# The branch for experts with more than 256 rows, moved from ahead of the last expert to the beginning of the experts

## The chip, the cores and the metric

One NeuronCore of a Trainium2 chip runs the whole program. The metric is the device time of one execution in microseconds (us). The engines are named as the profile names them: PE is TensorE's matmuls and PEld its weight loads (one sequencer issues both), DVE is VectorE, ACT is ScalarE, POOL is GpSimd, SP is SyncE. A "q" behind a name (PEldq, SPq) marks work of that engine's sequencer, such as a branch or a wait, during which the engine itself may go on with what is queued.

## The reference, cut to what matters

Three stages in a row: a blocked linear attention, a gated product of dense matrices, and a top-1 mixture of eight experts on 1536 rows of 512. Only the last one matters here (capacity is 1536 / 8 * 2 = 384 rows for an expert):

```python
for i in range(N):
    e = expert_idx[i]
    if counts[e] < capacity:
        disp[e, counts[e]] = x[i]
        pos[i] = counts[e]; counts[e] += 1; keep[i] = True
h = np.maximum(np.einsum('ecd,edf->ecf', disp, w1), 0.0)
y = np.einsum('ecf,efd->ecd', h, w2)
for i in range(N):
    if keep[i]:
        out[i] = gate_w[i] * y[expert_idx[i], pos[i]]
```

## The kernel before, in words

**Rows and chunks.** An expert may get up to 384 rows, three chunks of 128 (`nch` = 3). The straight path computes the first two chunks of every expert (`nmain` = 2, 256 rows). A branch holds the third chunk of all eight experts: `overflow()` loads the largest count of rows, `cmax`, into a register of every engine, and its body runs only where that is over 256. In the run that is shown the body is not taken. In the body TensorE has, for each of the eight experts, four transposes (L850), 32 matmuls (L863) and 8 matmuls (L876) in plain float32.

**The order is written by hand.** Each engine runs its instructions in the order of the program's text, and waits on semaphores. Around the change the order is this.

1. The last rows of the dense product: `half_b` and `half_a` for blocks 9 to 11 (L807 to L811), with `advance` and `table` hooked in between their matmuls. `advance` steps the routing of a block: its second step adds the block's one-hot rows to `csum` (L609), the third adds to the table of places. `table` turns that into row indices and starts the gathers of the second halves of the rows of experts 0 and 1 (POOL, L708). A hook is called behind the step `fb` of the same number, and there are steps 0 to 7: the hook at 8 in `half_a(NBLK - 2, {8: advance})` is never called, and stands there so that no `advance` runs behind the half.
2. `x2_half(NBLK - 1, ...)` (L812), the last half block, with `dispatch(0, 1, apart=True)` behind its step 6: four transposes on TensorE (L757), whose results ACT rounds to the high part (`xh`, L769) and DVE turns into the low part (`xl`, L770). Then `rows_a` copies and stores the last rows (L636, L637), and POOL gathers the first halves for experts 0 and 1, which wait for that store.
3. The count: one matmul of `ones` with `csum` (L817) and a DVE maximum to `cmax` (L819).
4. The beginning of the experts (L823 to L830): `mm1(e, pr, (2, 3))` is the second half of the inner sum of the first product, 12 matmuls; it runs for `pr` 0 to 3 of expert 0 and 0 to 1 of expert 1, with `dispatch(1, 1)` and `dispatch(0, 0)` between. The other half, `mm1(0, pr, (0, 1))`, is the first thing in the loop over experts and needs `dispatch(0, 0)`.
5. The loop over experts (L887 on): the rest of `mm1`, the dispatch and gathers for the next experts, then the second product with `e2` (L906) for both chunks and a scatter of the rows by POOL (L718).

**The weights** come in a fixed order through four staging buffers (SP's queue, L82), and ACT (L95) and DVE (L97) split each piece into a high and a low part in `run_bg` steps that stand between the matmuls.

**The branch.** On each engine it is a load of `cmax` by the sequencer (L833, TENSOR_LOAD) and a compare and branch (L834). Where the body is not taken, each engine's other side raises the semaphores by what the body would have added: PE and DVE one instruction each, SP one for each of eight DMA semaphores and POOL one for all of its own (INC_SWDGE_SEM), the last two after a wait for what is still in flight on them. In the kernel before it stands ahead of expert 7 (`OVER`, L888).

Of the kernel before, what the change touches and what calls it, by code (L numbers as in the profile page):

```python
# [12 lines left out]
I32 = mybir.dt.int32  # L13
AF = mybir.ActivationFunctionType
ALU = mybir.AluOpType
AX = mybir.AxisListType
PSUM = bass.MemoryType.PSUM

P = 128
# [4 lines left out]
NE = 8  # L24
NC = 6
NBLK = NT // P
# [5 lines left out]
NST = 4  # L32
NW = (2, 1, 1, 1, 1, 1, 1, 1)
HOOK = 6
OVER = 7
LOADS = (1, 2, 2, 2, 2, 2, 2, 0)
TICKS = ((0, 0, 0, 0), (0, 0, 0, 1)) + ((1, 0, 0, 1),) * 6 + ((0, 0, 1, 0),)
XBW = 265
# [3 lines left out]
def tile_moe_chain(ctx, tc, cap, qk, kv, w12, w3i, woi, wgi, e1i, e2i, c32, c16, zero, out):  # L42
    nc = tc.nc
    nch = min(-(-cap // P), NBLK)
# [6 lines left out]
    def pool(name, bufs=1, **kw):  # L51
        return tc.tile_pool(name=name, bufs=bufs, reuse_waits="tile", **kw)

    const = ctx.enter_context(pool("const"))
# [9 lines left out]
    def bank():  # L64
        return ps.tile([P, 512], F32, tag="b", name="bank")
# [140 lines left out]
    def run_bg(n=1):  # L206
        for _ in range(n):
            feed.tick()
# [70 lines left out]
    csum = const.tile([P, NE], F16, name="csum")  # L279
# [14 lines left out]
    def mm3(acc, wh, wl, rh, rl, first, last):  # L294
        nc.tensor.matmul(acc, wh, rl, start=first, stop=False)  # L295
        nc.tensor.matmul(acc, wh, rh, start=False, stop=False)  # L296
        nc.tensor.matmul(acc, wl, rh, start=False, stop=last)  # L297
# [248 lines left out]
    ones = c16_sb[:, 128:256]  # L546
# [24 lines left out]
    def x2_half(blk, cs, hooks={}):  # L571
        g, tb = divmod(blk, 3)
        ts = slice(tb * P, (tb + 1) * P)
        acc = bank()[:, 0 : cs.stop - cs.start]
        for fb in range(8):
            gh, gl = gts[g, fb]
            mm3(acc, gh[:, ts], gl[:, ts], wxh[:, fb, cs], wxl[:, fb, cs], fb == 0, fb == 7)
            if fb in hooks:
                hooks[fb]()
        return acc  # L580
# [53 lines left out]
    def rows_a(blk, acc):  # L634
        row = p2.tile([P, 256], F32, tag="rowa", name="rowa")
        nc.scalar.copy(row, acc)  # L636
        nc.scalar.dma_start(xa_d[blk * P : (blk + 1) * P, :], row)  # L637
# [5 lines left out]
    def advance():  # L643
        for r in list(routing):
            if next(r, 0) == 0:
                routing.remove(r)

    def half_b(blk, hooks={}):
        acc = x2_half(blk, slice(256, 520), hooks)
        if not hooks:  # L650
            advance()
        routing.append(route(blk, acc))
        next(routing[-1])
        if not hooks:
            run_bg(1)

    def half_a(blk, hooks={}):
        acc = x2_half(blk, slice(0, 256), hooks)
        if not hooks:
            advance()  # L660
        rows_a(blk, acc)
        run_bg(1)
# [64 lines left out]
    def gathers(e, half):  # L727
        for s in range(nmain):
            gather(xg[e % 2][s][half], (xa_d, xb_d)[half], s * NE + e)
# [15 lines left out]
    def dispatch(e, half, apart=False):  # L745
        if e not in xd:
            xd[e] = (
                p3.tile([P, 4, nt], F32R, tag="xdh", name="xdh"),
                p3.tile([P, 4, nt], F32R, tag="xdl", name="xdl"),
                p3.tile([P, nmain], F32, tag="gate", name="gate"),  # L750
            )
        xh, xl, gt = xd[e]
        tp = psi.tile([P, 512], F32, tag="i", name="tp") if half else bank()
        tps = [tp[:, 0:nt], bank()[:, 0:nt] if apart else tp[:, nt : 2 * nt]]
        for kk in range(2):
            for s in range(nmain):
                nc.tensor.transpose(  # L757
                    tps[kk][:, s * P : (s + 1) * P],
                    xg[e % 2][s][half][:, kk * P : (kk + 1) * P],
                    ident,  # L760
                )
        k = 2 * half
        if apart:
            parts = [(xh[:, k + n, :], xl[:, k + n, :], tps[n]) for n in range(2)]
        else:
            tp = tp[:, 0 : 2 * nt].rearrange("p (k t) -> p k t", k=2)
            parts = [(xh[:, k : k + 2, :], xl[:, k : k + 2, :], tp)]
        for h, lo, src in parts:
            nc.scalar.copy(h, src)  # L769
            nc.vector.tensor_tensor(lo, src, h.bitcast(F32), op=ALU.subtract)  # L770
        if half:
            for s in range(nmain):
                nc.vector.tensor_copy(gt[:, s : s + 1], xg[e % 2][s][1][:, 264:265])

    def mm1(e, pr, ks):
        xh, xl, _ = xd[e]
        it = e1_it[2 * e + pr // 2]
        feed.need(it, pieces=2 * (pr % 2) + 2)
        if ks[0] == 2:
            accs[e, pr] = bank()[:, 0 : 2 * nt]  # L780
        acc = accs[e, pr]
        for m in range(2):
            hi, lo = (it.by_fb(part, (2 * pr + m) % 4) for part in (it.hi, it.lo))
            o = acc[:, m * nt : (m + 1) * nt]
            for k in ks:
                for w, x in ((hi, xl), (hi, xh), (lo, xh)):
                    nc.tensor.matmul(  # L787
                        o,
                        w[:, k, :],
                        x[:, k, :],  # L790
                        start=m == 0 and k == 2 and x is xl,
                        stop=m == 1 and k == 1 and w is lo,
                        skip_group_check=True,
                    )
        if ks[-1] == 1:
            hh = p3h.tile([P, 2, nt], F32R, tag="hh", name="hh")
            hl = p3h.tile([P, 2, nt], F32R, tag="hl", name="hl")
            acc = accs.pop((e, pr)).rearrange("p (m t) -> p m t", m=2)
            nc.scalar.activation(hh, acc, AF.Relu)  # L799
            nc.vector.scalar_tensor_tensor(  # L800
                hl, acc, 0.0, hh.bitcast(F32), op0=ALU.max, op1=ALU.subtract
            )
            hts[pr] = (hh, hl)
            it.free = pr % 2 == 1
        run_bg(2 if ks[-1] == 1 else 1)

    half_b(NBLK - 3, {8: advance})  # L807
    half_b(NBLK - 2, {4: advance})
    half_b(NBLK - 1, {4: advance})
    half_a(NBLK - 3, {3: advance, 6: advance, 7: table})  # L810
    half_a(NBLK - 2, {8: advance})  # L811
    acc = x2_half(NBLK - 1, slice(0, 256), {HOOK: lambda: dispatch(0, 1, apart=True)})  # L812
    rows_a(NBLK - 1, acc)
    gathers(0, 0)
    gathers(1, 0)
    cnt = bank()[:, 0:NE]
    nc.tensor.matmul(cnt, ones, csum, start=True, stop=True)  # L817
    cmax = const.tile([P, 1], I32, name="cmax")
    nc.vector.tensor_reduce(cmax, cnt, axis=AX.X, op=ALU.max)  # L819

    late.close()
    p3h = ctx.enter_context(pool("p3h", 6, side="right"))
    hts = {}  # L823
    for pr in range(4):
        mm1(0, pr, (2, 3))
        if pr == 1:
            dispatch(1, 1)
    mm1(1, 0, (2, 3))
    dispatch(0, 0)
    mm1(1, 1, (2, 3))  # L830

    def overflow():
        nmax = nc.values_load(cmax[0:1, 0:1], min_val=0, max_val=NT)  # L833
# [50 lines left out]
                    scatter(y, col)  # L884

    ov = ctx.enter_context(pool("ov", side="right")) if nch > 2 else None
    for e in range(NE):  # L887
        if nch > 2 and e == OVER:  # L888
            overflow()
        for pr in range(4):  # L890
            mm1(e, pr, (0, 1) if (e, pr) in accs else (2, 3, 0, 1))
        gt = xd.pop(e)[2]
        if e + 1 < NE:
            if e:
                dispatch(e + 1, 1)
            dispatch(e + 1, 0)
        if e + 2 < NE:
            gathers(e + 2, 1)
            gathers(e + 2, 0)
        for s in range(nmain):  # L900
            acc = bank()
            ss = slice(s * P, (s + 1) * P)
            for fb in range(8):
                it = e2_it[2 * e + fb // 4]
                feed.need(it)
                mm3(  # L906
                    acc,
                    hts[fb // 2][0][:, fb % 2, ss],
                    hts[fb // 2][1][:, fb % 2, ss],
                    it.view(it.hi)[:, fb % 4, :],  # L910
                    it.view(it.lo)[:, fb % 4, :],
                    fb == 0,
                    fb == 7,
                )
                it.free = s == nmain - 1 and fb % 4 == 3
                if fb % 2:
                    run_bg(1)
            y = p3.tile([P, DM], F32, tag="y", name="y", bufs=3)
            cut = DM if (e, s) != (NE - 1, nmain - 1) else DM // 2
            nc.scalar.activation(y[:, 0:cut], acc[:, 0:cut], AF.Copy, scale=gt[:, s : s + 1])  # L920
            if cut < DM:
                nc.vector.tensor_scalar(
                    y[:, cut:], acc[:, cut:], gt[:, s : s + 1], None, op0=ALU.mult
                )
            scatter(y, s * NE + e)
# [69 lines left out]
```

## Time and profile before

| | us |
|---|---|
| median of three runs (513.02 to 513.99) | 513.52 |
| the profiled execution's own time | 516.84 |
| span of its trace, first to last instruction | 514.8 |

Busy time in that span: PE 498.6 us, PEld 468.7, DVE 264.9, ACT 242.9, POOL 128.7. TensorE's granted clock has a mean of 0.997 of full speed.

All times in the rows below are of the profiled execution, counted from the start of its span. A time of a run without the profiler is some 3.3 us under the profiled execution's own, so differences are worked out inside the trace and then set against the median. Matmuls overlap in the records (each is longer than its distance to the next), so what a matmul costs is the distance from start to start.

### The profile page before, as it was taken

The numbers are of one execution on the slowest core, as the hardware profiler recorded it, in microseconds if no ns is written. First come the engines' busy times: TensorE is split into PE (matmuls) and PEld (weight loads), VectorE is DVE, ScalarE is ACT, GpSimd is POOL, SyncE is SP. The second block draws the span as 40 slices with busy tenths as digits, with TensorE's granted clock in tenths as the row PEclk, the third lists the DMA queues.
The fourth block names the chain that finished last, engine by engine and source line by source line (L and its number), as shares of the span: only waits on it lengthen the run. The fifth ranks groups of instructions, "written<-read, shape, count | busy, mean of one in ns | idle before, by whom it ended". The sixth has DMA issues, their size and how long they took to land. (4 is left out here: it accounts for less than half of the span.)

```text
span 514.8 us, 9557 instructions
## 1 busy us (share of the span) xinstructions
PE 498.6 (97%) x3805; PEld 468.7 (91%) x3805; DVE 264.9 (51%) x576; ACT 242.9 (47%) x485; POOL 128.7 (25%) x124
## 2 busy tenths in 40 slices
PE   8999999999999999999999998899999999999993
PEld 4888999999999999999999998789989898989892
DVE  5998875668332223222332563468383746547420
ACT  2697997789311221122112424457464746546310
POOL 4365664545100000000020005405414040410101
PEclk9999999999999999999999999999999999999998
DMA  8999565557801000100010224486666666574200
GB/s 325 413 410 375 155 227 204 189 187 247 320 26 41 1 0 23 43 1 0 23 43 0 88 69 157 162 299 219 214 213 211 224 224 228 177 250 171 83 2 34
DMA packets 24529, 80.80 MB, mean 157 GB/s; under 512 B 3642, under 2 KB 5692, under 8 KB 24480
## 3 DMA queue, kind: packets, MB, share of 16 engines
q1 hardware_dynamic: 18976, 70.35, 38.4%
q0 software_dynamic: 3344, 7.85, 4.8%
q10 hardware_dynamic: 2160, 1.94, 1.1%
q8 instruction: 32, 0.52, 0.4%
q14 instruction: 17, 0.14, 0.1%
HBM read 74.84 MB, written 10.54 MB: 166 GB/s over the span
## 5 line engine op out<-in xcount | busy, mean ns | idle before, releaser
L97 DVE TENSOR_TENSOR wlo<-st,whi 128x512 fp32r<-128x512 f32 x128 | 82.0, 684 | 16.7 <-ACT whi L95 16.7
L295 PE MATMUL bank<-xtl,whi 128*128 128x384 f32 x256 | 87.1, 340 | 0.0
L297 PE MATMUL bank<-xth,wlo 128*128 128x384 f32 x256 | 86.4, 337 | 0.0
L296 PE MATMUL bank<-xth,whi 128*128 128x384 f32 x256 | 85.8, 335 | 0.0
L95 ACT CAST whi<-st 128x512 fp32r<-128x512 f32 x128 | 73.1, 621 | 16.2 <-PE bank L297 10.7
L787 PE MATMUL bank<-xdl,whi 128*128 128x256 f32 x256 | 72.6, 283 | 4.7 <-issue 2.5
L787 PE MATMUL bank<-xdh,whi 128*128 128x256 f32 x256 | 72.2, 282 | 0.0
L787 PE MATMUL bank<-xdh,wlo 128*128 128x256 f32 x256 | 72.1, 282 | 0.0
L143 POOL TENSOR_TENSOR wlo<-t,whi 128x512 fp32r<-128x512 f32 x40 | 51.9, 1298 | 52.1 <-ACT whi L142 46.5
L295 PE MATMUL bank<-wxl,gh 128*128 128x264 f32 (+1 forms) x192 | 55.9, 291 | 0.0
L296 PE MATMUL bank<-wxh,gh 128*128 128x264 f32 (+1 forms) x192 | 54.1, 282 | 0.0
L297 PE MATMUL bank<-wxh,gl 128*128 128x264 f32 (+1 forms) x192 | 54.1, 282 | 0.0
L787 PEld LDWEIGHTS bank<-xdl,whi 128*128 128x128 f32 x256 | 48.4, 189 | 5.6 <-issue 2.7
L564 DVE TENSOR_TENSOR a_sb<-bank,a_sb 128x384 f32<-128x384 f32 x32 | 17.8, 557 | 66.9 <-PE bank L297 66.3
L295 PE MATMUL bank<-wlo,hh 128*128 128x512 f32 x128 | 51.1, 399 | 0.0
L297 PE MATMUL bank<-whi,hl 128*128 128x512 f32 x128 | 50.4, 394 | 0.0
L718 POOL DMA_INDIRECT out_dram<-y,idx x16 | 16.6, 1038 | 134.2 <-ACT y L920 101.1
L296 PE MATMUL bank<-whi,hh 128*128 128x512 f32 x128 | 50.0, 391 | 0.0
L800 DVE SCALAR_TENSOR_TENSOR hl<-bank,hh 128x512 fp32r<-128x512 f32 x32 | 22.1, 690 | 53.3 <-ACT hh L799 45.5
L787 PEld LDWEIGHTS bank<-xdh,whi 128*128 128x128 f32 x256 | 48.3, 189 | 0.3
L787 PEld LDWEIGHTS bank<-xdh,wlo 128*128 128x128 f32 x256 | 48.4, 189 | 0.0
L295 PEld LDWEIGHTS bank<-xtl,whi 128*128 128x128 f32 x256 | 48.1, 188 | 0.0
(109 smaller groups left out, 1006.1 us busy)
## 6 DMA issues: line engine op xcount, KB each, us to landing
st<-e1i SPq DMA_DIRECT2D x32, 512.0 KB
st<-e2i SPq DMA_DIRECT2D x32, 512.0 KB
st<-w3i SPq DMA_DIRECT2D x16, 512.0 KB
st<-w SPq DMA_DIRECT2D x16, 512.0 KB
tqk<-qk SPq DMA_DIRECT2D x8, 768.0 KB
tkv<-kv SPq DMA_DIRECT2D x8, 768.0 KB
st<-woi SPq DMA_DIRECT2D x8, 512.0 KB
out_dram<-zero SPq DMA_DIRECT2D x1, 3072.0 KB
```

The costliest lines, as they stand in the source:

```text
L95: nc.scalar.copy(h, s)
L97: nc.vector.tensor_tensor(lo, s, h.bitcast(F32), op=ALU.subtract)
L143: nc.gpsimd.tensor_tensor(lo, t, h.bitcast(F32), op=ALU.subtract)
L295: nc.tensor.matmul(acc, wh, rl, start=first, stop=False)
L296: nc.tensor.matmul(acc, wh, rh, start=False, stop=False)
L297: nc.tensor.matmul(acc, wl, rh, start=False, stop=last)
L564: nc.vector.tensor_tensor(a_sb, acc, a_sb, op=ALU.mult)
L718: nc.gpsimd.indirect_dma_start(out=out, out_offset=bass.IndirectOffsetOnAxis(ap=idx[:, col : col + 1], axis=0), in_=src, in_offset=None, b ...
L787: nc.tensor.matmul(o, w[:, k, :], x[:, k, :], start=m == 0 and k == 2 and x is xl, stop=m == 1 and k == 1 and w is lo, skip_group_check=True,)
L800: nc.vector.scalar_tensor_tensor(hl, acc, 0.0, hh.bitcast(F32), op0=ALU.max, op1=ALU.subtract)
```

## The change

The count moves up, behind step 2 of `half_a(NBLK - 2)`; by then `csum` has its last addition, which stands in `half_a(NBLK - 3)`. It replaces the hook that is never called. The branch moves from ahead of expert 7 to right behind `rows_a`, ahead of the gathers of the first halves and of all matmuls of the experts; its body is unchanged. Every engine's stream is touched at both places.

```diff
-OVER = 7
...
+    cmax = const.tile([P, 1], I32, name="cmax")
+
+    def count():
+        cnt = bank()[:, 0:NE]
+        nc.tensor.matmul(cnt, ones, csum, start=True, stop=True)
+        nc.vector.tensor_reduce(cmax, cnt, axis=AX.X, op=ALU.max)
+
...
-    half_a(NBLK - 2, {8: advance})
+    half_a(NBLK - 2, {2: count})
     acc = x2_half(NBLK - 1, slice(0, 256), {HOOK: lambda: dispatch(0, 1, apart=True)})
     rows_a(NBLK - 1, acc)
-    gathers(0, 0)
-    gathers(1, 0)
-    cnt = bank()[:, 0:NE]
-    nc.tensor.matmul(cnt, ones, csum, start=True, stop=True)
-    cmax = const.tile([P, 1], I32, name="cmax")
-    nc.vector.tensor_reduce(cmax, cnt, axis=AX.X, op=ALU.max)
-
     late.close()
     p3h = ctx.enter_context(pool("p3h", 6, side="right"))
-    hts = {}
-    for pr in range(4):
...
-    mm1(1, 1, (2, 3))
...
     ov = ctx.enter_context(pool("ov", side="right")) if nch > 2 else None
+    if nch > 2:
+        overflow()
+    gathers(0, 0)
+    gathers(1, 0)
+    hts = {}
+    for pr in range(4):
+        mm1(0, pr, (2, 3))
+        if pr == 1:
+            dispatch(1, 1)
+    mm1(1, 0, (2, 3))
+    dispatch(0, 0)
+    mm1(1, 1, (2, 3))
     for e in range(NE):
-        if nch > 2 and e == OVER:
-            overflow()
         for pr in range(4):
```

## Rows read from the trace of the kernel before

**Rows 1.** The page: busy time, share of the span, instructions of each engine.
```profile
PE 498.6 (97%) x3805; PEld 468.7 (91%) x3805; DVE 264.9 (51%) x576; ACT 242.9 (47%) x485; POOL 128.7 (25%) x124
```

**Rows 2.** Waits of PE from 315 us to the end: total, times, longest (us).
```profile
PE bank L787 <- issue: 2.5, 1, 2.5
```

**Rows 3.** Timeline ahead of expert 7: start, length (us), instruction, idle before.
```profile
482.82 0.39 PE L297 MATMUL bank<-whi,hl 128*128 128x512 f32 x1
...
483.98 0.19 PEld L787 LDWEIGHTS bank<-xdl,whi 128*128 128x128 f32 x1 [1.19 <-PEq L834]
...
484.20 0.28 PE L787 MATMUL bank<-xdh,whi 128*128 128x256 f32 x1
```

**Rows 4.** Timeline ahead of expert 6, at the same place without a branch.
```profile
459.53 0.40 PE L297 MATMUL bank<-whi,hl 128*128 128x512 f32 x1
...
459.88 0.27 PE L787 MATMUL bank<-xdh,whi 128*128 128x256 f32 x1
```

**Rows 5.** Lines L833, L834: minimum/median/maximum ns, first to last start (us).
```profile
L833 PEldq TENSOR_LOAD <-cmax x1: 492/492/492, 478.9 to 478.9; - x1
L834 PEldq COMPARE_BRANCH  x1: 4148/4148/4148, 479.5 to 479.5; - x1
L834 DVEq COMPARE_BRANCH  x1: 72/72/72, 482.3 to 482.3; - x1
L834 POOLq INC_SWDGE_SEM  x1: 1332/1332/1332, 487.8 to 487.8; - x1
```

**Rows 6.** DMA at 304.18:304.21, 320.25:320.28, 478.60:478.65, 481.28:481.33, 484.40:484.43, 491.20:491.23 (packets, MB, share of 16 engines).
```profile
q8 instruction: 1, 0.02, 275.4%
...
q8 instruction: 1, 0.02, 187.5%
...
q8 instruction: 1, 0.02, 129.8%
...
q8 instruction: 1, 0.02, 109.9%
...
q8 instruction: 1, 0.02, 194.2%
...
q8 instruction: 1, 0.02, 217.1%
```

**Rows 7.** Windows: busy us and instructions (x) of PE, PEld, DVE, ACT, POOL; PEclk.
```profile
304.19:314.55 10.36, 10.36 (x92) 10.00 (x90) 4.05 (x18) 2.57 (x7) 4.15 (x5) 1.00 0.43 134
304.19:320.26 16.07, 14.73 (x129) 14.37 (x128) 6.43 (x26) 5.41 (x14) 6.15 (x7) 1.00 0.44 140
478.62:482.83 4.21, 4.21 (x21) 3.42 (x19) 1.99 (x3) 1.99 (x4) 0.98 (x1) 1.00 0.26 93
484.41:491.21 6.80, 6.80 (x59) 6.80 (x58) 2.47 (x4) 1.71 (x3) 0.78 (x1) 1.00 0.07 28
```

**Rows 8.** Timeline of PEld at the new place of the branch.
```profile
313.52 0.25 PEld L757 LDWEIGHTS tp<-c_sb,xgb 128*128 128x128 f32 x2
...
315.89 0.19 PEld L787 LDWEIGHTS bank<-xdl,whi 128*128 128x128 f32 x1 [1.43 <-DVE xdl L770]
```

**Rows 9.** Timeline around the dispatch of expert 0's first half.
```profile
323.59 0.60 PE L757 MATMUL bank<-c_sb,xga 128*128 128x128 f32 x4
...
327.37 0.69 DVE L770 TENSOR_TENSOR xdl<-bank,xdh 128x512 fp32r<-128x512 f32 x1 [4.64 <-issue]
...
328.12 0.39 PE L787 MATMUL bank<-xdl,whi 128*128 128x256 f32 x1 [2.51 <-issue]
```

**Rows 10.** Timeline of POOL: the first gather behind the new place.
```profile
317.93 1.00 POOL L708 DMA_INDIRECT xga<-xa_d,idx  x1 [3.73 <-DMA xa_d<-rowa]
```

**Rows 11.** Timeline and windows on TensorE's clock: the first matmuls, and the end.
```profile
1.19 5.25 PE L325 MATMUL bank<-warm 128*128 128x512 f16 x12 [1.19 <-DVE warm L319]
...
506.80:511.40 4.60, 0.00 (x0) 0.00 (x0) 0.48 (x1) 0.47 (x1) 0.98 (x1) 1.00 0.10 39
...
511.45:514.80 3.35, 0.00 (x0) 0.00 (x0) 0.00 (x0) 0.00 (x0) 0.00 (x0) 0.50 0.00 0
```

More of the change, by code (lines that the diff above doesn't have):

```diff
@@ L810, in tile_moe_chain @@
     half_a(NBLK - 3, {3: advance, 6: advance, 7: table})
-    half_a(NBLK - 2, {8: advance})
+    half_a(NBLK - 2, {2: count})
     acc = x2_half(NBLK - 1, slice(0, 256), {HOOK: lambda: dispatch(0, 1, apart=True)})
     rows_a(NBLK - 1, acc)
-    gathers(0, 0)
-    gathers(1, 0)
-    cnt = bank()[:, 0:NE]
-    nc.tensor.matmul(cnt, ones, csum, start=True, stop=True)
-    cmax = const.tile([P, 1], I32, name="cmax")
-    nc.vector.tensor_reduce(cmax, cnt, axis=AX.X, op=ALU.max)
     late.close()
     p3h = ctx.enter_context(pool("p3h", 6, side="right"))
-    hts = {}
-    for pr in range(4):
[L825 to L829, printed above, removed]
-    mm1(1, 1, (2, 3))
     def overflow():
```

## The prediction, made before the changed kernel ran

> **What bounds the kernel now.** The page comes first: TensorE is busy for 97% of the span and nothing else is near it [rows 1], so a change is worth what it adds to or takes from TensorE's stream. The view of waits says where that stream stands still among the experts: three places only. One wait of 2.5 us [rows 2] is that of `mm1(0, 0, (0, 1))`, which starts at 328.12 because `dispatch(0, 0)` ended its last subtraction then [rows 9]. One of 1.43 us lies ahead of the first `mm1` at 315.89, for `dispatch(0, 1)` [rows 8]. The third is the branch, ahead of expert 7 [rows 3]. The change touches all three.
>
> **What goes: the branch ahead of expert 7.** With the branch, the second matmul of `mm1` starts 484.20 - 482.82 = 1.38 us behind the last matmul of the expert before [rows 3]; at the same place ahead of expert 6 it is 459.88 - 459.53 = 0.35 us [rows 4]. The branch costs 1.03 us there. It is TensorE alone that holds it up: its compare and branch took 4148 ns, DVE's 72 ns [rows 5]. From here to the last matmul TensorE has no other gap, so 1.03 us comes back whole. The other engines' parts at that place lie beside TensorE's work, and their going brings nothing.
>
> **Why TensorE's branch takes 4.15 us.** The sequencer starts it at 479.55 and is through at 483.70. Queue q8 carries single instruction packets of 0.02 MB. Between 304.2 and 320.25 one comes in the time of 129 + 128 = 257 TensorE instructions [rows 6, 7]: a block of some 256 instructions each. At the branch they come out of turn: one at 478.6 (129.8% of 0.05 us times 16 engines = 1.04 us long), one at 481.3, 1.75 us into the branch (0.88 us long, ended 482.2), one at 484.4 (0.93 us), 0.7 us behind the landing [rows 6]. I read it so: the body that is jumped over is longer than what is held, the landing's block is fetched and can be used 1.5 us behind its packet (482.2 to 483.7), and then the block behind it is asked for. The fetch started only when the one of 478.6 could be used (479.65 + 1.5 = 481.2). Ahead of expert 7 most of the 4.15 us is hidden: the load of `cmax` started at 478.9, while the last matmul queued ahead of it started at 482.82 [rows 3, 5], so 3.9 us of 512-column matmuls were in the queue.
>
> [...]
>
> **What comes: the branch at 314 us.** TensorE's sequencer waits for a gather and lets `dispatch(0, 1)`'s transposes go at 313.52 [rows 8]; ahead of the branch are then four transposes and three matmuls, 14 instructions, at most 0.06 us each. So almost nothing is queued when it gets to the branch. The steps:
> - `cmax` is loaded from about 313.8 (313.6 to 314.3), 0.49 us [rows 5]; the branch starts at 314.4 (314.2 to 314.9).
> - First fetch. No packet is under way (304.2, next 320.25 [rows 6]), so it need not wait for another one: 0.7 + 0.93 + 1.52 = 3.15 us, between 3.05 (with the 0.88 us packet) and the measured 4.15. I take 3.15, the composition of the packet at 484.4. Landing at 317.55; the first weight load 0.28 us later (483.70 to 483.98 [rows 3]).
> - Where it lands. Ahead of expert 7, 40 instructions are counted from the packet at 478.62 to the branch [rows 7], about 37 without those that had started; the sequencer is 33 entries ahead of the engine, and a packet follows its request by some 0.6 us, 5 instructions there. The branch is then some 11 instructions into its block (with the two of the branch itself). At the new place 177 instructions lie between the packet at 304.2 and the last matmul ahead (92 + 90, less three under way and the count's pair [rows 7]); 177 - 33 + 2 + 10 = 156. The body is 8 * (4 + 2 * 40) pairs, 1344 instructions (a plain float32 matmul runs as two pairs), and 1371 with waits and branch in the compiled program: 1372 further is five blocks and 92. So the landing moves from 103 to 248. Counted from behind, by the packets at 484.4 and 491.2 (117 instructions between [rows 7]), the old landing is at 112, which makes the new one 257. The end of the block, 256, lies inside that bound. I take the last few instructions of a block, as the mean, 252, says.
> - Second fetch. The block behind is asked for when the landing is reached, and TensorE has no more than a few instructions until it is there: another 3.15 us (0.7 + 0.93 + 1.52), to 320.7. `mm1` runs from 320.75 instead of 315.89: 4.86 us late, 4.4 at the least and 6.3 at the most with the bounds above.
> - What hides it. Of this, the wait at 328.12 takes 2.51 us [rows 9]: the next 9.7 us of matmuls need nothing new but `dispatch(0, 0)`, whose transposes (323.59) move along to 328.4; with 0.6 us for the transposes, 0.6 for ACT and 0.69 for DVE its parts are there at about 330.4, when `mm1(1, 1)` ends (325.6 + 4.86). What is late next is nothing else. Left: 4.86 - 2.51 = 2.35 us (1.9 to 3.8).
> - The clock. TensorE would stand from 314.5 to 320.7 but for a few instructions. [...] If it falls, matmuls of 512 columns come every 0.43 us, as at the start (12 in 5.25 us [rows 11]), not every 0.23; over a stretch as long as that first one the loss is 5.0 * (1 - 0.23 / 0.43) = 2.3 us. [...]
>
> **What costs nothing, and what covers it.** POOL's part waits for the gathers in flight and takes 1.33 us [rows 5]; its cover is the 3.73 us that POOL waits for the row store ahead of the next gather at 317.93 [rows 10]. If the cover were gone, that gather's rows are needed only by the transposes at 323.59, 5.7 us behind its issue, and at 328.4 in the new order. SP's part waits for its loads to land and delays the next weight load by a microsecond or two; four staging buffers are between. ACT and DVE each load `cmax` too, about 0.5 us, ahead of weight splits that TensorE, late itself, needs later. The count's matmul and maximum move ahead, and are done long before the branch.
>
> **Sum**: -1.03 + 2.35 + 1.2 = +2.5 us. The trace's span would be 517.3 and that execution 519.3; set against the median of 513.52, it is 516.0 us.
>
> **Rivals.**
> - *The landing is in the first few instructions of the next block, one fetch* (27%). Then `mm1` runs from 317.8 (317.5 to 319.3), 1.9 us late (1.6 to 3.4), against 2.51 us of wait that it eats: 0 to 0.9 us is left, and the sum is -1.03 to -0.1 us, 512.5 to 513.4; I take 512.5. For it: the count from behind, 257. Against: the count from ahead, 248. The point that decides is the landing's place in its block, 256.
> - *TensorE's branch is held until its queue is empty, not by a fetch* (10%). The last matmul ended at 483.21 and the branch at 483.70. At the new place it would end about 0.5 us behind the last matmul, 315.05, and the weight load 0.28 later is still ahead of 315.89: no cost, sum -1.03 us, 512.5. Against it: DVE's branch took 72 ns with a subtraction running, and the packet at 481.3 came only 2.7 us behind the one before. [...]
> - *The stall reaches further* (8%): both fetches take 4.15 us or the clock falls for longer, and the sum passes +4.7 us, 518.2.
>
> **How the numbers follow.** 55% for the forecast, whose own range is 513.52 + 0.85 (4.4 - 2.51 - 1.03, full clock) to 518.6 (6.3 - 2.51 - 1.03 + 2.3), 514.4 to 518.6. The range for 8 in 10 reaches to the rivals on the fast side, whose likely value is 512.5, and leaves out the far end of the slow side: 512.4 to 518.0. About 1.03 us, 0.2%, is what a measurement of this kernel can tell from no change. Slower by more than that: nearly all of the forecast and the last rival, 0.58. Within it: half of the two fast rivals, whose 1.03 us lies on the edge, and the low end of the forecast, 0.24. Faster: 0.18.
>
> **What would show it.** In the changed trace: TensorE's branch at about 314.4 with 3 to 4 us; two q8 packets behind it, some 3 us apart; `mm1` beginning with a few instructions at 317.8 and going on at 320.7; no wait of 2.5 us ahead of `mm1(0, 0, (0, 1))`; a granted clock of 0.50 for some microseconds, or not; 0.35 us ahead of expert 7 as ahead of expert 6. One stall alone makes the landing wrong; no stall, the fetch; a wait for a gather or for weights in that stage, what I cost at nothing.

## The result, and the profile after

The changed kernel took 520.38 us in the median of four runs (519.07 to 520.86), the kernel before 513.44: ratio 1.0135, 95% interval 1.0123 to 1.0147. It is slower by 6.9 us; the prediction had +2.5 us (516.0, range 512.4 to 518.0). The direction is right, the size is not.

The page of the changed kernel (busy time, share of the span, instructions) and its view of waits (line, releaser: total us, times, longest), against [rows 1, 2]:

```profile
PE 500.4 (97%) x3805; PEld 470.9 (91%) x3805; DVE 265.2 (51%) x576; ACT 242.7 (47%) x485; POOL 127.7 (25%) x124
```

```profile
PE bank L786 <- PEq L825: 3.5, 1, 3.5
PE bank L786 <- issue: 1.8, 1, 1.8
```

The wait of 2.5 us for `dispatch(0, 0)` is gone, and so is that of 1.4 us ahead of the first `mm1`. Two others stand in their place, both at the branch's new place. The timeline of PE there (start, length, instruction, idle time before), where [rows 8, 9] show the kernel before:

```profile
313.53 0.38 PE L756 MATMUL tp<-c_sb,xgb 128*128 128x128 f32 x2
...
314.20 0.28 PE L296 MATMUL bank<-wxh,gl 128*128 128x256 f32 x1
318.01 0.55 PE L786 MATMUL bank<-xdl,whi 128*128 128x256 f32 x1 [3.53 <-PEq L825]
318.36 0.42 PE L786 MATMUL bank<-xdh,whi 128*128 128x256 f32 x1
318.58 0.41 PE L786 MATMUL bank<-xdh,wlo 128*128 128x256 f32 x1
318.79 0.41 PE L786 MATMUL bank<-xdl,whi 128*128 128x256 f32 x1
321.02 0.58 PE L786 MATMUL bank<-xdh,whi 128*128 128x256 f32 x1 [1.81 <-issue]
...
324.38 0.28 PE L786 MATMUL bank<-xdh,whi 128*128 128x256 f32 x1
...
324.98 0.60 PE L756 MATMUL tp<-c_sb,xgb 128*128 128x128 f32 x4
```

TensorE stands for the branch, does four matmuls, stands again without a semaphore to wait for ("issue"), and then a matmul comes every 0.21 us until 324.38, and every 0.12 us from there. The line of the branch (minimum/median/maximum ns, first to last start), against [rows 5], and two q8 packets in windows of 0.08 and 0.10 us (75.5% of 16 engines in 0.08 us is 0.97 us; 80.4% in 0.10 is 1.29), against [rows 6]:

```profile
L825 PEldq COMPARE_BRANCH  x1: 3552/3552/3552, 314.1 to 314.1; - x1
L825 DVEq COMPARE_BRANCH  x1: 72/72/72, 315.3 to 315.3; - x1
...
L825 POOLq INC_SWDGE_SEM  x1: 496/496/496, 315.9 to 315.9; - x1
```

```profile
q8 instruction: 1, 0.02, 75.5%
...
q8 instruction: 1, 0.02, 80.4%
```

The packets start at 315.18 and 318.36. The windows (span, then busy us and instructions of PE, PEld, DVE, ACT, POOL, then PEclk, the granted clock, with DMA share and GB/s):

```profile
317.69:321.02 3.33, 1.20 (x5) 0.94 (x5) 0.00 (x0) 0.00 (x0) 2.24 (x3) 0.50 0.54 194
321.02:324.30 3.28, 3.28 (x15) 3.28 (x16) 0.00 (x0) 0.00 (x0) 2.67 (x3) 0.50 0.31 86
324.40:330.00 5.60, 5.60 (x49) 5.60 (x49) 2.61 (x6) 2.15 (x4) 1.00 (x1) 1.00 0.32 113
```

The granted clock is 0.50 from 317.55 to 324.37. Ahead of expert 7 the second matmul of `mm1` now starts 0.34 us behind the last matmul of the expert before, as in [rows 4]:

```profile
486.20 0.39 PE L296 MATMUL bank<-whi,hl 128*128 128x512 f32 x1
...
486.54 0.29 PE L786 MATMUL bank<-xdh,whi 128*128 128x256 f32 x1
```

So nearly every step of the working is to be seen in the trace, and the two profiles even differ by what was forecast: spans of 514.8 and 517.2 us, +2.4. The runs differ by 6.9, so that agreement is no success: it holds between these two executions alone. The profiled execution of the kernel before had taken 516.84 us, 3.3 more than its other runs, and that of the changed kernel 519.07, 1.3 less than its median. The first question is which of the two is not typical.

### The profile page after: what moved, and what is told of

The parts are those of the page before. It is cut to its first block, busy times and chain, and to the rows that moved or that the text cites. A ratio compares the mean times of both kernels' runs of the same rounds, so it can differ in the third digit from the quotient of the medians.

```text
span 517.2 us, 9555 instructions
## 1 busy us (share of the span) xinstructions
PE 500.4 (97%) x3805; PEld 470.9 (91%) x3805; DVE 265.2 (51%) x576; ACT 242.7 (47%) x485; POOL 127.7 (25%) x124
## 3 DMA queue, kind: packets, MB, share of 16 engines
q10 hardware_dynamic: 2160, 1.94, 1.1%
```

## The experiments

Each ratio is to runs of the kernel before that were taken along with the experiment (medians of 513.12 to 513.44 us).

**1. The kernel before, profiled a second time.** No edit.

> The kernel before, unchanged, for a second profiled execution of it. The first took 516.84 us while three runs shown took 513.02 to 513.99. Theory A (the first profile of the kernel before held a stall that its other executions don't have, so the 2.51 us that I counted as slack at 328.12 is not there): its own time is 513.0 to 514.0 us, its span about 511.5, and TensorE has no wait of over 1 us ahead of mm1(0, 0, (0, 1)). Theory B (the stall is in every execution and the changed kernel lost its extra 4 us somewhere else): the wait of about 2.5 us is there again.

Measured: 513.27 us (eight runs), ratio 0.9995 (0.9985 to 1.0005); the profiled execution took 513.28, its span is 511.1. Its waits from 313 us to the end, and its timeline where [rows 8, 9] had two standstills:

```profile
PE bank L787 <- PEq L834: 0.9, 1, 0.9
PE bank L787 <- DVE xdl L770: 0.3, 1, 0.3
```

```profile
313.24 0.73 PE L757 MATMUL tp<-c_sb,xgb 128*128 128x128 f32 x2
...
314.88 0.39 PE L787 MATMUL bank<-xdl,whi 128*128 128x256 f32 x1 [0.33 <-DVE xdl L770]
...
317.84 0.60 PE L757 MATMUL tp<-c_sb,xgb 128*128 128x128 f32 x4
...
322.56 0.60 PE L757 MATMUL bank<-c_sb,xga 128*128 128x128 f32 x4
323.19 0.59 ACT L769 CAST xdh<-bank 128x512 fp32r<-128x512 f32 x1 [2.57 <-PE bank L757]
323.81 0.69 DVE L770 TENSOR_TENSOR xdl<-bank,xdh 128x512 fp32r<-128x512 f32 x1 [2.10 <-ACT xdh L769]
```

Theory A holds. The subtraction of `dispatch(0, 0)` is done 1.94 us behind the start of its transposes (322.56 to 324.50), not 4.47 as in [rows 9], and nothing waits for it. The wait ahead of the first `mm1` is 0.33 us (of the matmuls; [rows 8] has 1.43 for the weight loads). What I had counted as slack was a delay of that one execution. The 3.3 us between the first profile's own time and the median, which the section on the time before puts down to the profiler, are that execution's too: the second one, profiled like it, took 513.28 us, in the middle of its runs (512.72 to 513.91). None of the later profiles of kernels with this order, here and below, has it.

**2 and 3. No branch at all, in either order.** In the first, the kernel before without the call; in the second, the changed kernel without it (both leave out the third chunks' body).

```diff
-        if nch > 2 and e == OVER:
-            overflow()
```

```diff
-    if nch > 2:
-        overflow()
```

> The kernel before without its branch (the body for experts with more than 256 rows is left out altogether; the count stays). My step 1 says the branch ahead of expert 7 costs 1.03 us: 0.998 of the time before, 512.4 us. If the branch was hidden in ordinary executions, the time is that of before, 513.4.

> The changed kernel without its branch (body left out): the count stands in the second half-a, gathers behind it. If all of the loss is the branch (theories A and B both), this equals the kernel before without its branch, 512.4 us within 0.3. If the earlier count or the shifted gathers cost something by themselves, it is slower than that by that much, up to the 4 us that my sum lacks.

Measured: 512.48 us, ratio 0.9986 (0.9976 to 0.9995), and 512.21, ratio 0.9980 (0.9970 to 0.9990). The old branch is worth 0.3 to 1.2 us in the one, 0.5 to 1.5 in the other; my 1.03 lies in both. Moving the count and the gathers costs nothing. So the whole loss, 8 us against the same order without it, belongs to the branch at its new place.

**4. One block further.** The changed kernel with a body longer by 24 TensorE instructions, which never run:

```diff
+PAD = 6
...
+                    if e == NE - 1:
+                        pad = bank()[:, 0:P]
+                        for k in range(PAD):
+                            nc.tensor.matmul(pad, xdt[:, 0, :], xdt[:, 1, :], start=k == 0, stop=k == PAD - 1)
```

> The changed kernel with six more float32 matmuls (24 TensorE instructions) in the untaken body, so that the landing moves from the last few instructions of its block of 256 into the next block by about 16. Step 4 of the prediction (landing in the end of a block makes a second fetch): one fetch of about 3.2 us at 314.4, mm1 runs on from 317.8, no second standstill of 1.8 us; with the slack of 2.51 us gone (theory A) the loss is 1.9 - 1.03 = 0.9 us and what the clock takes, 514.3 to 515.5 us; with the slack there (theory B) 512.5 to 513. If the second standstill has nothing to do with the landing's place, the time stays at 520.4.

Measured: 517.98 us, ratio 1.0090 (1.0074 to 1.0107). Its waits and timeline of PE (its lines stand one further down, by `PAD`):

```profile
PE bank L787 <- PEq L826: 3.5, 1, 3.5
```

```profile
318.16 0.36 PE L787 MATMUL bank<-xdl,whi 128*128 128x256 f32 x1 [3.52 <-PEq L826]
...
318.95 0.34 PE L787 MATMUL bank<-xdl,whi 128*128 128x256 f32 x1
319.08 0.42 PE L787 MATMUL bank<-xdh,whi 128*128 128x256 f32 x1
...
322.29 0.36 PE L787 MATMUL bank<-xdh,whi 128*128 128x256 f32 x1
322.49 0.28 PE L787 MATMUL bank<-xdh,wlo 128*128 128x256 f32 x1
```

The second standstill is gone: it came from the landing's place in its block, as the fourth step has it. 2.4 us come back. The time is over the 514.3 to 515.5 us that I expected, for two reasons. The first `mm1` is 318.16 - 314.88 = 3.3 us late against the second profile of the kernel before, not 1.9. And the clock falls here too (0.50 from 319.08 to 322.40), after 3.5 us of standing: 16 matmuls take 3.41 us (319.08 to 322.49) instead of 16 * 0.119 = 1.90, a loss of 1.5 us.

**5. A short body.** The changed kernel with the body for expert 0 alone (the other seven are left out):

```diff
-            for e in range(NE):
+            for e in range(1):
                 for s in range(2, nch):
```

> The changed kernel with the body for expert 0 alone (the seven other experts' part of the untaken branch is left out): 172 TensorE instructions to jump over instead of 1372. Theory F (the stall is the fetch of a landing that is not held): the landing is in the block behind the branch's own, which is there already; TensorE's branch takes under 0.5 us, no packet of q8 comes out of turn, and the time is that without a branch, 512.2 to 512.7 us. Theory Q (TensorE's branch is held by a queue that has to drain, by the other engines, or by the price of a branch as such): it takes 3.5 us as before, and the time stays at 518 to 520.4.

Measured: 513.60 us, ratio 1.0008 (0.9999 to 1.0018). The branch, and the first `mm1`:

```profile
L825 PEldq COMPARE_BRANCH  x1: 352/352/352, 314.9 to 314.9; - x1
L825 DVEq COMPARE_BRANCH  x1: 72/72/72, 315.9 to 315.9; - x1
```

```profile
316.33 0.35 PE L786 MATMUL bank<-xdl,whi 128*128 128x256 f32 x1 [1.17 <-DVEq L825]
```

With nothing changed but the length of what is jumped over, TensorE's branch takes 0.35 us and not 3.55, and the ratio falls from 1.0135 to 1.0008: 6.5 of the 6.9 us are gone. That is the fetches, with the fall of the clock behind them; that TensorE's branch is held by a queue that has to drain, by the other engines, or by a price of a branch as such, is ruled out. One q8 packet still comes, at 315.96, 0.75 us behind the branch's end, and nothing waits for it; that fits my reading, a landing in a block that is held, with the block behind it asked for. The time is still some 1 us above my forecast. `mm1` starts only behind VectorE's own way through the branch (its comparison at 315.93), although `xdl`, which it reads first, was ready at 315.45 (its subtraction starts at 315.03 and takes 424 ns). VectorE's load of `cmax` starts at 315.32, while that subtraction runs, and takes 0.54 us. This is a second, smaller cost of about 0.8 us, and I take it that the fetch hides it in the changed kernel, where `mm1` starts later than that.

**6. Cover for the fetch.** The changed kernel with 16 matmuls ahead of the branch, into a bank that nobody reads:

```diff
+    wk = bank()
+    for _ in range(16):
+        nc.tensor.matmul(wk, ones, c16_sb[:, 0:512], start=True, stop=True)
     late.close()
```

> The changed kernel with 16 more matmuls (512 columns, f16, into a bank that nobody reads; 32 instructions) ahead of the branch. They move the landing into the next block (one fetch, as with the longer body, 518.0 us) and keep TensorE busy while that fetch runs. If the clock's fall is what the longer body's profile shows (15 matmuls of mm1 every 0.214 instead of 0.119 us, 1.4 us), there is no half clock at 318 and the time is 516.3 to 516.8. If the fall has another cause than the standstill, the clock falls all the same and the time is 518.0 or more.

Measured: 516.89 us, ratio 1.0068 (1.0052 to 1.0085). Timeline of PE, and a window over the branch and the first matmuls of the experts:

```profile
314.81 3.63 PE L822 MATMUL bank<-c_sb 128*128 128x512 f16 x16
319.57 0.35 PE L786 MATMUL bank<-xdl,whi 128*128 128x256 f32 x1 [1.14 <-PEq L828]
```

```profile
314.00:330.00 16.00, 14.80 (x108) 12.46 (x109) 6.16 (x14) 5.33 (x11) 7.91 (x9) 1.00 0.46 145
```

The clock does not fall (1.00), and there is one standstill, as the landing is in the next block. The median is 1.1 us below that of the longer body, although the fetch of the profiled execution took 0.6 us more (4.07 us; its packet was 1.67 us long). The two profiled executions don't show that difference (516.89 and 516.66 us), because that of the longer body was 1.3 us under its median. The clock fell where TensorE had stood for 3.5 us (experiment 4) and didn't where it stood for 1.14 us: matmuls that do nothing held it.

**7 and 8. Other places of the old branch.** `OVER = 6` and `OVER = 5` in the kernel before.

> The kernel before with its branch one expert earlier, ahead of expert 6. By the changed kernel's trace a block ends 12 instructions behind its landing; counted from there, the old branch (ahead of expert 7) stood 4 instructions into its block, so that the fetch of the next block was under way and its own had to wait. Ahead of expert 6 it is 209 into its block and lands 45 into another. Theory F: one fetch of 3.0 to 3.5 us behind 3.9 us of queued matmuls, nothing shows; 1.0 us less than before, 0.998, 512.3. If 1 us is the price of a branch ahead of any expert, 513.3.

> The kernel before with its branch ahead of expert 5: 158 into its block by the same count, landing 250 into another, 6 ahead of its end, as at the changed kernel's place. Theory F: the first fetch is hidden behind 3.9 us of queued matmuls, a second one of 3.1 us follows behind a few instructions with 0.4 to 0.9 us still queued: TensorE stands 2.2 to 2.7 us in mm1(5, 0), 514.5 to 515.5 us in all, more if the clock falls. If the landing's place doesn't matter, it equals the branch ahead of expert 6 or of expert 7.

Measured: ahead of expert 6 514.14 us, ratio 1.0016 (0.9998 to 1.0033); ahead of expert 5 519.86, ratio 1.0131 (1.0114 to 1.0148). The branch of each, first expert 6, then expert 5, and for expert 5 the timeline of PE and the granted clock behind the second standstill:

```profile
L834 PEldq COMPARE_BRANCH  x1: 4472/4472/4472, 453.1 to 453.1; - x1
```

```profile
L834 PEldq COMPARE_BRANCH  x1: 5932/5932/5932, 429.0 to 429.0; - x1
```

```profile
435.22 0.35 PE L787 MATMUL bank<-xdl,whi 128*128 128x256 f32 x1 [2.50 <-PEq L834]
437.87 0.58 PE L787 MATMUL bank<-xdh,whi 128*128 128x256 f32 x1 [2.29 <-issue]
```

```profile
437.60:440.90 3.30, 3.03 (x14) 3.03 (x15) 0.00 (x0) 0.00 (x0) 0.43 (x1) 0.50 0.07 22
```

My forecast for expert 6 was wrong: the branch is no cheaper there, and it takes 4.47 us, where I had 3.0 to 3.5. For expert 5 the landing does what the count of instructions said (one matmul, then a second standstill of 2.29 us; I had 2.2 to 2.7), but the first fetch takes 5.93 us, 2.5 us more than its cover; and the clock falls (0.50). The forecast of 514.5 to 515.5 is 4.4 us short. What the branch's time is made of, from the q8 packet in each (us):

| profile | branch starts | packet starts behind it | packet takes | branch ends behind the packet | branch takes |
|---|---|---|---|---|---|
| changed | 314.14 | 1.04 | 0.97 | 1.54 | 3.55 |
| changed, second profile | 315.09 | 0.94 | 0.97 | 1.50 | 3.41 |
| longer body | 314.30 | 1.14 | 0.94 | 1.39 | 3.47 |
| cover | 315.18 | 1.04 | 1.67 | 1.36 | 4.07 |
| before, second profile | 475.77 | 1.74 | 0.91 | 1.50 | 4.15 |
| ahead of expert 6 | 453.09 | 2.08 | 1.03 | 1.36 | 4.47 |
| ahead of expert 5 | 428.98 | 1.65 | 2.90 | 1.38 | 5.93 |
| behind the last expert (experiment 10) | 498.61 | 1.21 | 1.48 | 1.40 | 4.09 |

The last part is steady. The wait for the packet and the packet itself are not. Traffic alone does not explain the packet's length: the DMA share during the branch is 0.82 ahead of expert 5 and 0.85 ahead of expert 6, where the packet took 1.03 us, and 0.15 with the cover, where it took 1.67 (0.21 in the changed kernel). Ahead of expert 6 no earlier packet was under way (the one before is at 436.87), and it took longest to start. So the late start at the old place need not be an earlier fetch, as I had read it. What sets the two parts stays open; no run here varied the weight loads alone.

**9. The changed kernel, profiled again.** No edit.

> The changed kernel, unchanged, for a second profile and more times. Its first profile took 519.07 us, the least of its four runs. Its parts against the second profile of the kernel before: mm1 first starts 2.84 us later, stands 1.81 us once more and runs 20 matmuls at 0.214 instead of 0.119 us (1.9 us), 1.05 us come back ahead of expert 7. If the other runs differ only by where the clock's fall begins and by how long the packets take, the profile shows the same two standstills, 3.4 to 4.2 and 1.8 to 2.5 us, and the time is 520 to 521. If the first profile was the odd one, one standstill is missing or a third appears.

Measured: 520.50 us, ratio 1.0140 (1.0125 to 1.0154), span 518.8. The time and the second standstill are as expected, the first (3.43 us) too, with a wait for a gather ahead of it:

```profile
314.49 0.33 PE L756 MATMUL tp<-c_sb,xgb 128*128 128x128 f32 x1 [0.53 <-DMA xgb<-xb_d,idx]
...
318.82 0.35 PE L786 MATMUL bank<-xdl,whi 128*128 128x256 f32 x1 [3.43 <-PEq L825]
...
321.56 0.58 PE L786 MATMUL bank<-xdh,whi 128*128 128x256 f32 x1 [2.04 <-issue]
...
326.00 0.91 PE L756 MATMUL tp<-c_sb,xgb 128*128 128x128 f32 x4
```

**10. The branch behind the last expert.** The kernel before with `overflow()` after the loop.

```diff
-        if nch > 2 and e == OVER:
-            overflow()
...
             scatter(y, s * NE + e)
+    if nch > 2:
+        overflow()
```

> The branch behind the last expert, where TensorE has nothing left to do (a version that might beat both). If a branch costs only what TensorE waits for, the time is that without a branch, 512.3 to 512.5 us. If the other engines' ways through the branch (GpSimd's wait for the last scatter, SP's for its loads) come behind the last scatter, the tail grows by 1 to 3 us, 513.5 to 515.5.

Measured: 516.55 us, ratio 1.0067 (1.0054 to 1.0080), over both of my forecasts. No gain: TensorE is done, but GpSimd's branch waits for the last scatter to land (a semaphore of 2432 ns) and then 1380 ns more, both ahead of its part of the program's end:

```profile
L834 POOLq EVENT_SEMAPHORE  x4: 17/42/2432, 504.5 to 507.1; - x4
...
L834 POOLq INC_SWDGE_SEM  x1: 1380/1380/1380, 507.2 to 507.2; - x1
```

**11. The short body at the old place.** The edit of experiment 5, in the kernel before.

> The kernel before, its branch ahead of expert 7, with the body for expert 0 alone (the seven others' part of the untaken branch is left out). The landing is then 175 instructions behind the branch, in the same block. If the 1.03 us there are what the 3.9 us of queued matmuls leave of a fetch of 4.15 us and its restart, TensorE's branch takes under 0.5 us, nothing stands still and the time is 512.3 to 512.5 us, 0.998 of before. If it is the join of the engines, 1.0 us stays and the time is that of before.

Measured: 513.27 us, ratio 1.0006 (0.9997 to 1.0014), not the 512.3 to 512.5 that I expected. Its branch, its wait, and the timeline of PE:

```profile
L834 PEldq COMPARE_BRANCH  x1: 236/236/236, 476.4 to 476.4; - x1
L834 PEldq EVENT_SEMAPHORE  x1: 51/51/51, 480.1 to 480.1; - x1
```

```profile
PE bank L787 <- PEq L834: 0.3, 1, 0.3
```

```profile
479.72 0.39 PE L297 MATMUL bank<-whi,hl 128*128 128x512 f32 x1
480.40 0.35 PE L787 MATMUL bank<-xdl,whi 128*128 128x256 f32 x1 [0.30 <-PEq L834]
480.60 0.28 PE L787 MATMUL bank<-xdh,whi 128*128 128x256 f32 x1
```

TensorE's branch takes 236 ns, with over 3 us of matmuls still queued, so it does not wait for the queue. But the raise of the semaphore behind it does: the branch is over at 476.68, the raise (EVENT_SEMAPHORE) starts at 480.15, when the last queued matmul ends (479.72 and 0.39). The second matmul of `mm1` starts 0.88 us behind that last matmul. With the fetch it was 1.38 and, in the second profile, 1.46; without a branch 0.35 [rows 4]. So of the 1.03 us that I put down to the branch ahead of expert 7, about half is not the fetch, and a short body leaves it. This is read from one trace; no run here varied the raise.

In the times the runs show no gain. The interval leaves room for 0.15 us, while the profiles differ by 0.5 to 0.6 at the branch; why stays open, as these are amounts by which single executions scatter.

No version tried beats both kernels. The kernels without any branch, which leave out the third chunks, are 0.14 to 0.20% below the kernel before, so a better place for the branch can hardly bring more.

## Why the prediction was right in its direction and wrong in its size

The account, in us. The two profiles of the changed kernel are set against the second profile of the kernel before, by the starts of the same matmuls (first transposes; first `mm1`; fifth matmul of `mm1`; the transposes at 330.37 in that profile, 337.52 and 338.87 in the two; end of the span):

| term | predicted | first profile | second profile |
|---|---|---|---|
| first transposes later | 0 | 0.29 | 0.45 |
| first standstill (to the first `mm1`) | in 4.86 | 2.84 | 3.48 |
| second standstill (to its fifth matmul) | in 4.86 | 2.43 | 2.17 |
| rest of the stage at the lower clock | 1.2 | 1.59 | 2.39 |
| taken by the wait at 328.12 | -2.51 | 0 | 0 |
| from there to the end (branch gone) | -1.03 | -1.11 | -0.78 |
| sum | +2.5 | +6.04 | +7.71 |

The mean of the two sums is 6.9 us, the measured loss; with two executions, of which the first was the fastest of its four, that they meet it so closely is in part luck. The 3.48 holds 0.4 us of the wait for a gather (the second pair of transposes starts 0.96 us behind the first, against 0.56).

The steps, counted in the order of the prediction, from what goes (1) to what costs nothing (7):

- *The branch's old price* (step 1) and *0.35 us ahead of expert 7*: as forecast in the changed profile, 0.34 us.
- *The branch is a fetch* (step 2): right; experiment 5 shows it by taking the fetch away. The reading of why it took 4.15 us at the old place (an earlier packet to wait for) is not borne out by the branch ahead of expert 6. And only about half of the 1.03 us at the old place is the fetch (experiment 11).
- *The length of the jump.* With 172 instructions to jump over TensorE's branch took 352 ns (236 at the old place), with 1372 it took 3412 to 3552 at the new place. From which length on it takes microseconds, no run shows.
- *Times at the new place* (step 3): branch at 314.14 for 3.55 us against 314.4 and 3.15; landing at 317.69 against 317.55. The 0.06 us an instruction is an estimate from 117 instructions in 6.80 us [rows 7].
- *The landing in the last instructions of a block, and a second fetch* (step 4): right. Four matmuls, then a standstill until 321.02 (320.75 forecast). Experiments 4 and 8 move the landing, and the second standstill (1.81 and 2.04 us in the changed kernel, 2.29 in experiment 8) goes and comes with it. The counts rest on the trace of the kernel before: 33 instructions of TensorE, 17 matmuls and 16 weight loads, start behind the start of the load of `cmax` (478.95); a plain float32 matmul is two pairs (192 matmul records for the 96 calls of L391); a block of 256 is an estimate from the 257 of [rows 6, 7]; and the 0.6 us from a request to its packet is one from the 0.7 us between the landing and the packet at 484.4.
- *What hides it* (step 5): this is the step that failed. Of the 4.86 us, "the wait at 328.12 takes 2.51 us", I wrote [rows 9]. In the second profile of the kernel before it is not there: from the first transposes to those behind the wait (333.94 and 330.37) is 3.3 us less. Nothing was there to eat the standstill. That alone is 2.5 of the 4.4 us that I was short. In that profile the first `mm1` starts 1.64 us behind its transposes, not the 2.34 (315.89 - 313.55) of [rows 8], so the standstill takes 0.7 us more.
- *The clock* (step 6): it fell, and I had taken half a fall. No run shows the 1.2 us of the sum, which was my choice between no fall and the 2.3 us of my estimate; the runs showed 1.6 to 2.4. 15 matmuls behind the second standstill ran at the lower level (a granted clock of 0.50, one every 0.214 us) in the one profile, 20 and the transposes in the other. In the first profile the four matmuls between the standstills did too, 0.4 us that the table has in the second standstill. The trace of the kernel before has two standstills to compare: over the 2.51 us ahead of 328.12, and from there to 334, the granted clock is 1.00; behind the last matmul it is 1.00 for 4.6 us, and 0.50 from there [rows 11].
- *The other engines cost nothing* (step 7): right for the time of this kernel, by the cover of the fetch alone. SP's branch kept its next weight load until 318.10 (316.01 in the second profile of the kernel before). GpSimd's next gather started at 318.17 (317.93 before [rows 10], but 316.94 in that second profile), and what released it was SP, whose first raise came at 317.42, 7.0 us behind its comparison; with the short body it came 0.2 us behind. Why it took so long the runs don't show. VectorE's join would have shown with 0.8 us, had the fetch not.
- *The rivals*: one fetch alone is what experiment 4 built, 518.0 us, not the 512.5 I gave it, for the same two reasons (no slack, and a clock that falls). "Held until the queue is empty" is ruled out for the branch by experiments 5 and 11; the raise behind it is so held (experiment 11), which costs about half a microsecond at the old place. "The stall reaches further" had the nearest time, 518.2, with a mechanism that is half right: neither fetch took 4.15 us, but the clock did fall for longer than the 5.0 us of my estimate, 6.8 us. What put the time above it is the slack that was not there.

What made the delay of 2.5 us in the first profile of the kernel before stays open. Its trace has ScalarE starting on the transposes 3.2 us behind their start, where the second has 0.6, with no record that names a cause.

## What to carry to other kernels

Where a profiled execution is longer than the runs, ask which of its rows the runs don't have before a wait in it is counted as slack: here 3.3 us of difference stood on the page, and 2.5 of it was the very wait on which the sum leaned. Ahead of a branch over a long body, let wide matmuls fill TensorE's queue (ahead of expert 5 even they left 2.5 us of the fetch bare), and count where the jump lands (a second standstill of 1.8 to 2.3 us hung on it); or make the body short, which took 6.5 of 6.9 us away here. A standstill of TensorE is to be priced with the clock behind it (1.6 to 2.4 us here), and matmuls that do nothing can hold the clock (16 of them did in experiment 6, where it is 1.00).

## What the runs showed of the hardware that I had not expected

- The fetch is no constant: 3.41 to 5.93 us for a jump over the same body. Its packet of 0.02 MB takes 0.91 to 2.90 us and starts 0.94 to 2.08 us behind the branch, and the DMA share does not order them (0.82 with a packet of 2.90 us, 0.85 with one of 1.03, 0.15 with one of 1.67).
- The granted clock fell to 0.50 behind a standstill of 3.5 us (experiment 4); behind 2.5 us in the first profile of the kernel before it had not (1.00). In experiment 9 it was 1.00 from 315.00 to 318.80, over the first standstill, and 0.50 from 319.90, in the second, behind four matmuls 0.12 us apart; in the first profile of the changed kernel it fell at 317.55, in the first one.
- A branch whose body is not taken made engines wait for one another in three runs: behind it TensorE's first wait for VectorE's semaphore, 1.17 us, lasted until VectorE had gone through the branch as well (experiment 5), TensorE's own raise started only when its queue was empty (0.05 us behind the last matmul's end in experiment 11), and a branch at the end put a wait of 2.43 us for GpSimd's last scatter on the path (experiment 10).
